# Solved blocks turned ahead of the second gap, and three solves begun ahead of the third: a recurrent-attention and mixture-of-experts kernel on one core

## The chip, the core and the metric

The kernel runs on one core of one Trainium2 chip. The metric is the device time of an execution in microseconds; three runs of the kernel before took 1157.42, 1158.74 and 1160.82 us, median 1158.74 us. The profile is one further execution, taken by the hardware profiler, with a span of 1155.3 us.

The engines are named as the profile names them: PE is TensorE (PEld its weight loads), DVE is VectorE, ACT is ScalarE, POOL is GpSimd, SP is SyncE, which issues most transfers. Each runs its own queue of instructions, and semaphores tie the queues together.

## The reference

Two blocks follow each other. The first is a recurrence over 768 time steps for 4 batches of 8 heads with a head size of 40:

```python
for t in range(S):
    y[:, :, t] = np.einsum('bhd,bhde->bhe', rt, state)
    Sa = np.einsum('bhde,bhe->bhd', state, at)
    state_decay = state * wt[:, :, None, :] - np.einsum('bhd,bhe->bhde', Sa, bt)
    state = state_decay + np.einsum('bhd,bhe->bhde', vt, kt)
```

Its output, reshaped to x of 3072 tokens by 320, goes through four experts of width 1024, whose results are mixed with normalized probabilities:

```python
p = domain_probs / (domain_probs.sum(-1, keepdims=True) + 1e-09)
for e in range(E):
    h = np.maximum(x @ w1[e], 0.0)
    out += p[:, e:e + 1] * (h @ w2[e])
```

All of it is in float32.

## The kernel before

The time axis is cut into 12 chunks of 64 steps. A **unit** is one chunk of two of the four batches; there are 24 units, two to a chunk, numbered from 0 here. Within a chunk the recurrence becomes matrix products and a triangular system, one of 64 by 64 for each head and batch. A unit goes through four generators, each cut into parts by `yield`:

- `within(q)`: everything that needs no state. Its parts in order: decay products G; the reciprocal gp; the scaled tokens n_tok and k_tok, the turned A, V and R (AT, VT, RT); NT and KT; the causal scores pc; the **triangle products** pfe, which give F (the strictly triangular matrix of the system) and the right side's ET; the copy into ET; EV.
- `substitute(q, engine)`: the **solve**. It gathers F's 32 by 32 diagonal blocks, turns them into M, makes the first products, and then substitutes row pair by row pair into Z, on POOL for all units from the third on.
- `merge(q)`: the **turning** of the solved blocks (Qc, QTc) and then the two products pY and pQ that join the blocks of 32 to one of 64.
- `step(q)`: the part that reads and writes the state, with the products prn, psat, pxr, pdy.

The parts of `within`, `substitute` and `merge` that matter here:

```python
        # within(q), sixth part: triangle products
        pf = quadrants(p, 0, BY_TOKENS, L, ...)          # pfe<-NT,AT
        pe = quadrants(p, NJ * L, BY_TOKENS, L, ...)     # pfe<-AT,KT
        q.F = sb.tile([P, H, L], FP32, name="F", tag="F", bufs=2)
        for s in range(2):
            nc.scalar.copy(out=of_slot(q.F[:], s), in_=pf[s])
        yield

    def substitute(q, eng, between=None):
        blocks = sb.tile([P, H, Q], FP32, name="blocks")
        for i in range(P // Q):
            move = nc.scalar.copy if i >= 2 else nc.vector.tensor_copy
            tc.keep_in_program_order(move(out=blocks[quarter(i)], in_=q.F[...]))
        M = sb.tile([P, Q, Q], FP32, name="M")
        ins = nc.vector.transpose(out=M[:], in_=cols)
        tc.keep_in_program_order(ins)
        tc.keep_in_program_order(nc.vector.memset(on_diag, 0.0))
        ...                                  # two products on DVE, into Z and M, pinned
        for x in (0, 3) if at_once else (0,):
            tc.keep_in_program_order(eng.tensor_copy(out=Z[:, x], in_=unit_cols[:]))
        for j in range(0, Q, 2):             # 16 row pairs: one product, two sums each
            ins = eng.tensor_tensor(out=Z[:, 1:3, 0:n, j + 1:Q], ..., op=ALU.mult)
            ...
                for x in range(1, 3):
                    eng.tensor_tensor(out=z[:, 0], in0=z[:, 0], in1=z[:, x], op=ALU.add)

    def merge(q):
        tc.keep_in_program_order(nc.vector.transpose(out=dealt(Qc[:]), in_=q.Z))
        tc.keep_in_program_order(nc.vector.transpose(out=QTc..., in_=Qc...))
        q.QT = QTs()
        for i in range(P // Q):
            ins = nc.gpsimd.tensor_copy(out=q.QT[...], in_=QTc[quarter(i)])
            tc.keep_in_program_order(ins)
        yield
        ...                                  # pY<-QTc,F on PE, Yq on ACT
        yield
        ...                                  # pQ<-Yq,Qc on PE, QT on ACT
        yield
```

`keep_in_program_order` pins an instruction behind the one traced before it on the same engine. What isn't pinned may be moved by the scheduler that lays out each engine's queue when the kernel is built.

Between these run the **mixture pieces**, queued in `todo`: `up` (ph, then relu into hs), the products with the second weights (po, or p after a scheme with seven products of half size whose sums `a` are made by `add_h` on DVE), and the adds to the output tile `osb` on DVE. PSUM tiles of the mixture share three buffers (tag "mm"), those of the attention five (tag "big"). A **gap** is a place in a step where some of these pieces are put:

```python
    for u in range(1, NU):
        ...
        m, s_next = merge(units[u + 1]), begin_step(u + 1)
        w = ws[u + 2]                        # within of unit u + 2
        def gap(n, pieces=None):
            at = 4 * u + n
            run(sum_ops, sums_at.get(at, 0))
            mix((1 if at in sparse else 2) if pieces is None else pieces)

        run(w_next)
        run(s, 1)
        gap(0)
        early = u < 5
        if early:
            run(s, 1)
        run(w, 1)
        run(s)
        ...
        run(w, 1)
        gap(1)
        if not early:
            run(m, 1)                        # Qc, QTc of unit u + 1
        ...                                  # loads for unit u + 3
        run(w, 2)                            # NT, KT; causal scores
        if early:
            run(m, 1)
        else:
            run(s_next, 1)                   # prn
            run(m, 1)                        # pY
        gap(2)
        if not early:
            run(m, 1)
        run(w, 1)                            # triangle products
        if not early:
            run(s_next, 1)
        if u + 2 < NU:
            substitute(units[u + 2], nc.gpsimd)
        run(w, 1)                            # ET
        ...                                  # G of unit u + 3
        if early:
            run(m, 1)
            run(s_next, 1)
            run(m)
            gap(3, 1)
            run(s_next, 1)
            ...
        else:
            gap(3)
        s = s_next
```

Of the kernel before, what the change touches and what calls it, by code (L numbers as in the profile page):

```python
# [15 lines left out]
def kernel(  # L16
# [38 lines left out]
    nc = tc.nc  # L55
# [9 lines left out]
    NU = NC * B // 2  # L65
# [103 lines left out]
    units = []  # L169

    def begin(u):
        q = Unit()
        q.u, q.c, q.bp = u, u // (B // 2), u % (B // 2)
        q.b = [2 * q.bp, 2 * q.bp + 1]
        q.start, q.end = q.c == 0, q.c == NC - 1
        q.n = {}
        units.append(q)
        return q
# [38 lines left out]
    def go(moves, eng=None):  # L217
        for move in moves:
            move(eng or nc.sync)
# [99 lines left out]
    def quarter(q):  # L319
        return slice(Q * q, Q * q + Q)  # L320
# [190 lines left out]
# [5 lines that stand above are left out]
            tc.keep_in_program_order(move(out=blocks[quarter(i)], in_=q.F[quarter(i), :, quarter(i % 2)]))  # L516
        M = sb.tile([P, Q, Q], FP32, name="M")
        cols = blocks[:].rearrange("p h c -> p c h")[:, :, None, :].to_broadcast([P, Q, 4, H])
        ins = nc.vector.transpose(out=M[:], in_=cols)  # L519
        tc.keep_in_program_order(ins)  # L520


        pairs = M[:].rearrange("p (c two) r -> p c two r", two=2)
        on_diag = M[:].rearrange("p c r -> p (c r)")[:, Q + 1::2 * (Q + 1)]
        tc.keep_in_program_order(nc.vector.memset(on_diag, 0.0))

        Z = sb.tile([P, 4, Q // 4, Q], FP32, name="Z")
        q.Z = Z[:, 0]
        by_second = Z[:, 1:3].rearrange("p x k r -> p (x k) r")
        below = M[:].rearrange("p c r -> p (c r)")[:, 1::2 * (Q + 1)]  # L530
        ins = nc.vector.tensor_tensor(
            out=by_second, in0=pairs[:, :, 1, :], in1=below[:, :, None].to_broadcast([P, Q // 2, Q]), op=ALU.mult,
        )
        tc.keep_in_program_order(ins)
        ins = nc.vector.tensor_tensor(out=pairs[:, :, 0, :], in0=pairs[:, :, 0, :], in1=by_second, op=ALU.add)  # L535
        tc.keep_in_program_order(ins)
        run(between)
        at_once = eng is nc.vector
        for x in (0, 3) if at_once else (0,):
            tc.keep_in_program_order(eng.tensor_copy(out=Z[:, x], in_=unit_cols[:]))  # L540
        for j in range(0, Q, 2):
            n, m = j // 4 + 1, Q - 1 - j
            here = 3 * (j // 2 % 2) if at_once else 0
            ins = eng.tensor_tensor(  # L544
                out=Z[:, 1:3, 0:n, j + 1:Q], in0=M[:, j:j + 2, None, j + 1:Q].to_broadcast([P, 2, n, m]),
                in1=Z[:, here, 0:n, j:j + 2].rearrange("p k x -> p x k")[:, :, :, None].to_broadcast([P, 2, n, m]),
                op=ALU.mult,
            )
            if j == 0:
                tc.keep_in_program_order(ins)  # L550
            z = Z[:, :, 0:n, j + 1:Q]
            if at_once:
                terms = z[:, 0:3] if here == 0 else z[:, 1:4]
                eng.tensor_reduce(out=z[:, 3 - here], in_=terms.rearrange("p x k r -> p k r x"), op=ALU.add, axis=AX.X)
# [3 lines that stand above are left out]
        if at_once:  # L558

            odd, even = (Z[:, x].rearrange("p k (r four) -> p k r four", four=4)[:, :, :, 1:3] for x in (3, 0))  # L560
            eng.tensor_copy(out=even, in_=odd)

    def merge(q):


        Qc = sb.tile([P, H, Q], FP32, name="Qc", tag="q", bufs=2)
        QTc = sb.tile([P, H, Q], FP32, name="QTc", tag="q", bufs=2)
        tc.keep_in_program_order(nc.vector.transpose(out=dealt(Qc[:]), in_=q.Z))
        tc.keep_in_program_order(
            nc.vector.transpose(  # L570
                out=QTc[:].rearrange("p h r -> p (h r)"), in_=Qc[:].rearrange("p h c -> p (h c)"),
            )
        )
        q.QT = QTs()
        for i in range(P // Q):
            ins = nc.gpsimd.tensor_copy(out=q.QT[quarter(i), :, quarter(i % 2)], in_=QTc[quarter(i)])  # L576
            tc.keep_in_program_order(ins)
        yield

        py = big("pY")  # L580
        for h in range(H):
            for i in (1, 3):
                nc.tensor.matmul(
                    out=py[quarter(i - 1), h * Q:(h + 1) * Q], lhsT=q.F[quarter(i), h, 0:Q],
                    rhs=QTc[quarter(i), h, :], start=True, stop=True,
                )
        Y = sb.tile([P, H, Q], FP32, name="Yq")
        for i in (0, 2):
            nc.scalar.copy(out=Y[quarter(i)].rearrange("p h t -> p (h t)"), in_=py[quarter(i), 0:H * Q])
        yield  # L590

        pq = big("pQ")
        for h in range(H):
            for i in (0, 2):
                nc.tensor.matmul(  # L595
                    out=pq[quarter(i), h * Q:(h + 1) * Q], lhsT=Qc[quarter(i), h, :],
                    rhs=Y[quarter(i), h, :], start=True, stop=True,
                )
        for i in (0, 2):
            nc.scalar.copy(out=q.QT[quarter(i), :, quarter(1)], in_=by(pq[quarter(i), 0:H * Q], Q))  # L600
        yield
# [301 lines left out]
    def begin_later(n):  # L903
        for move in later[:n]:
            tc.keep_in_program_order(move(nc.sync))
        del later[:n]

    def mix(n):

        for piece in todo[:n]:  # L910
            piece()
            begin_later(3 if n > 1 else 6)
        del todo[:n]

    def run(gen, n=99):
        if gen is None:
            return
        for _ in range(n):
            if next(gen, gen) is gen:
                break  # L920
# [3 lines left out]
    def begin_step(u):  # L924
        q = units[u]
        if q.bp == 0:
            chunks_x[q.c] = sb.tile([P, 3, 2 * P], FP32, name="xT", tag="xT", bufs=2)
        q.xT = chunks_x[q.c][:, :, q.bp * P:(q.bp + 1) * P]
        return step(q, q.xT)
# [91 lines left out]
    for u in range(1, NU):  # L1021
        q = units[u]
        m = s_next = w = w_next = iter(())
        if u + 1 < NU:
            m, s_next = merge(units[u + 1]), begin_step(u + 1)
            w_next = ws[u + 1]
        if u + 2 < NU:
            w = ws[u + 2]
# [16 lines that stand above are left out]
        if u == 1:  # L1045
            mixture_of_unit(q)
        elif q.bp:
            mixture_of_chunk(units[u - 1:u + 1], chunks_x[q.c])
        begin_later(len(later))
        run(w, 1)  # L1050
        gap(1)
        if not early:
            run(m, 1)

        if u + 3 < NU:
            go(load_raw(begin(u + 3), "WA"))
            load(units[u + 3], "WBKV")
            later.extend(load_raw(units[u + 3], "VR"))
        run(w, 2)
        if early:  # L1060
            run(m, 1)
        else:
            run(s_next, 1)
            run(m, 1)
        gap(2)

        if not early:
            run(m, 1)
        run(w, 1)
        if not early:  # L1070
            run(s_next, 1)
        if u + 2 < NU:
            substitute(units[u + 2], nc.gpsimd)
        run(w, 1)
        if u + 3 < NU:
            ws.append(within(units[u + 3]))
            run(ws[u + 3], 1)
# [6 lines that stand above are left out]
            mix(0 if 4 * u + 3 in sparse else 1)  # L1084
# [3 lines that stand above are left out]
# [31 lines left out]
```

## Time and profile before

| | |
|---|---|
| median of 3 runs | 1158.74 us (1157.42 to 1160.82) |
| span of the profiled execution | 1155.3 us |
| mean granted TensorE clock | 0.984 |
| DVE waiting for POOL's solve, before Qc | 6.7 us in 3 waits |
| POOL waiting for M, before a solve | 312.3 us in 20 waits |

How the views are read. The page's first line gives each engine's busy time, its share of the span and its instructions. A line of waits reads: engine, tile and line that waited, `<-` what it waited for, then the total in us, the number of times and the longest. A line of a timeline reads: start in us, duration in us, engine, line of the kernel, operation, out `<-` in, partitions by elements, and how many were merged; in brackets stands the idle time of the engine just before, and what ended it. L371 is a helper that issues all products of 64 by 64, so those are told apart by their tiles.

### The profile page before, as it was taken

What the parts mean: (1) busy time and instruction counts of PE and PEld (TensorE: products, weight loads), DVE (VectorE), ACT (ScalarE), POOL (GpSimd) and SP (SyncE); (2) the same over time, 40 slices, a digit from 0 to 9 for tenths busy, and PEclk for the clock granted to TensorE, in tenths of its full rate; (3) what the DMA queues carried; (4) which work ended last, traced back from release to release, by engine and by line L of the source; (5) the groups of instructions that cost most, each with busy time, mean ns of one, the idle gap of its engine ahead of it and who ended that gap; (6) DMA issues with size and microseconds to landing.
All of it is one profiled execution on the core that took longest, in us unless ns stands there. A gap on an engine that the chain in (4) does not pass through costs nothing.

```text
span 1155.3 us, 38242 instructions
## 1 busy us (share of the span) xinstructions
PE 1103.2 (95%) x16036; PEld 979.6 (85%) x16036; DVE 757.6 (66%) x1553; ACT 341.3 (30%) x860; POOL 471.9 (41%) x1221
## 2 busy tenths in 40 slices
PE   6899997999999999999999999999999999999998
PEld 5777776888898888988888888888989888888887
DVE  8756547697677758757667667677577586543333
ACT  2323333333233232242332332332322323311110
POOL 4005627672633634625525526426336346340000
PEclk7899998999999999999999999999999999999999
DMA  7774643254364354454443443443543442231330
GB/s 120 215 227 125 133 97 77 69 126 101 77 149 95 89 125 113 103 121 104 108 118 80 122 115 84 117 97 87 134 104 88 114 110 62 75 89 52 104 91 12
DMA packets 268866, 122.16 MB, mean 106 GB/s; under 512 B 213736, under 2 KB 242072, under 8 KB 268696
## 3 DMA queue, kind: packets, MB, share of 16 engines
q1 hardware_dynamic: 265416, 119.12, 42.1%
q8 instruction: 126, 2.06, 0.8%
q10 hardware_dynamic: 3280, 0.61, 0.3%
q14 instruction: 44, 0.36, 0.1%
HBM read 111.79 MB, written 3.93 MB: 100 GB/s over the span
## 4 chain that ended last, share of the span: by engine, by line
PE 68%; DVE 17%; SPq 4%; POOL 3%; issue 3%; DMA 3%; ACT 2%; DVEq 0%; ACTq 0%; POOLq 0%
PE ph L734 24%; PE p L841 22%; PE ph L726 7%; DVE osb L752 3%; POOL Z L557 2%; PE pfe L371 2%; PE psat L371 2%; PE pxr L371 2%; SPq L711 2%; PE pdy L371 2%; PE po L775 2%; DVE gp L414 1%; DVE G L401 1%; SPq L205 1%; DVE a L835 1%
## 5 line engine op out<-in xcount | busy, mean ns | idle before, releaser
L734 PE MATMUL ph<-xT,w1p 128*128 128x256 f32 (+1 forms) x1520 | 343.8, 379 | 0.7 <-issue 0.7
L734 PEld LDWEIGHTS ph<-xT,w1p 128*128 128x128 f32 x1520 | 274.0, 190 | 63.6 <-issue 24.7
L544 POOL TENSOR_TENSOR Z<-M,Z 128x62 f32<-128x62 f32 (+7 forms) x352 | 144.6, 411 | 344.9 <-DVE M L535 312.3
L557 POOL TENSOR_TENSOR Z<-Z 128x31 f32<-128x31 f32 (+7 forms) x704 | 258.6, 367 | 55.2
L835 DVE TENSOR_TENSOR a<-hs 128x512 f32<-128x512 f32 x220 | 152.7, 711 | 156.7 <-ACT hs L739 156.7
L739 ACT ACTIVATE hs<-ph 128x512 f32<-128x512 f32 (+1 forms) x208 | 117.1, 564 | 325.1 <-PE ph L734 325.0
L841 PE MATMUL p<-sums,a 128*128 128x160 f32 x1056 | 165.1, 299 | 0.0
L752 DVE SCALAR_TENSOR_TENSOR osb<-p,gate,osb 128x320 f32<-128x320 f32 (+1 forms) x243 | 108.1, 482 | 85.0 <-PE p L841 80.5
L841 PEld LDWEIGHTS p<-sums,a 128*128 128x128 f32 x1056 | 152.9, 190 | 2.3
L726 PE MATMUL ph<-xT,w1p 64*128 64x256 f32 (+1 forms) x760 | 110.3, 398 | 0.9 <-issue 0.9
L576 POOL COPY QT<-QTc 32x256 f32<-32x256 f32 x96 | 46.9, 488 | 154.8 <-DVE QTc L570 151.0
L841 PE MATMUL p<-w,hs 128*128 128x160 f32 x704 | 102.9, 299 | 0.0
L841 PE MATMUL p<-w,a 128*128 128x160 f32 x704 | 102.8, 299 | 0.0
L841 PEld LDWEIGHTS p<-w,hs 128*128 128x128 f32 x704 | 100.3, 190 | 2.2
L841 PEld LDWEIGHTS p<-w,a 128*128 128x128 f32 x704 | 98.0, 190 | 0.0
L726 PEld LDWEIGHTS ph<-xT,w1p 64*128 64x128 f32 x760 | 68.0, 187 | 13.7 <-issue 3.8
L519 DVE STREAM_TRANSPOSE M<-blocks 128x1024 f32<-128x1024 f32 x24 | 47.0, 1957 | 24.2 <-ACT blocks L516 24.1
L414 DVE RECIPROCAL gp<-gp 128x320 f32<-128x320 f32 x24 | 51.7, 2152 | 0.8
L504 ACT COPY EV<-pev 64x160 f32<-64x160 f32 x96 | 23.4, 286 | 66.8 <-PE pev L371 66.4
L600 ACT COPY QT<-pQ 32x256 f32<-32x256 f32 x48 | 17.4, 363 | 85.0 <-PE pQ L595 84.4
L371 PE MATMUL pdy<-VC,k_tok 64*64 64x104 f32 (+1 forms) x768 | 41.4, 260 | 0.1
L371 PE MATMUL pdy<-SX,n_tok 64*64 64x104 f32 (+1 forms) x768 | 38.9, 247 | 1.1 <-DVE SX L382 1.1
(148 smaller groups left out, 1347.3 us busy)
## 6 DMA issues: line engine op xcount, KB each, us to landing
w1p<-in_moe_w_dram SPq DMA_DIRECT2D x95, 512.0 KB
w1p<-in_moe_w_dram SPq DMA_DIRECT2D x190, 64.0 KB
w<-in_moe_w_dram SPq DMA_DIRECT2D x4, 1280.0 KB
sums<-in_moe_w_dram SPq DMA_DIRECT2D x9, 512.0 KB
natW<-in_w_dram SPq DMA_DIRECT2D x48, 80.0 KB
natB<-in_b_dram SPq DMA_DIRECT2D x48, 80.0 KB
natK<-in_k_dram SPq DMA_DIRECT2D x48, 80.0 KB
out_dram<-osb SPq DMA_DIRECT2D x46, 80.0 KB
```

Of the source, the lines that this page charges most:

```text
L371: nc.tensor.matmul(out=p[row][half(col), lo + at * out_cols:lo + (at + 1) * out_cols], lhsT=lhsT, rhs=rhs, start=(n == 0), stop=(n == len( ...
L414: pin(nc.vector.reciprocal(out=gp[:], in_=gp[:]))
L519: ins = nc.vector.transpose(out=M[:], in_=cols)
L544: ins = eng.tensor_tensor(out=Z[:, 1:3, 0:n, j + 1:Q], in0=M[:, j:j + 2, None, j + 1:Q].to_broadcast([P, 2, n, m]), in1=Z[:, here, 0:n, j: ...
L557: eng.tensor_tensor(out=z[:, 0], in0=z[:, 0], in1=z[:, x], op=ALU.add)
L576: ins = nc.gpsimd.tensor_copy(out=q.QT[quarter(i), :, quarter(i % 2)], in_=QTc[quarter(i)])
L726: nc.tensor.matmul(out=ph[i][:, f, :], lhsT=w1.last[i * DT:(i + 1) * DT, f, :], rhs=xT[i * DT:(i + 1) * DT, 2, :], start=(f == 0), stop=False,
L734: nc.tensor.matmul(out=ph[i][:, f, :], lhsT=w1.main[:, g, at * P:(at + 1) * P], rhs=xT[:, g, :], start=False, stop=(g == 1 and f == HF // ...
L739: nc.scalar.activation(out=h[:, i * HF // 2:(i + 1) * HF // 2, 0:n], in_=ph[i][:], func=ACTF.Relu,)
L752: nc.vector.scalar_tensor_tensor(out=to, in0=p, scalar=sc, in1=to, op0=ALU.mult, op1=ALU.add)
L835: nc.vector.tensor_tensor(out=t[:], in0=x, in1=y, op=op)
L841: nc.tensor.matmul(out=p[:, n * HD:(n + 1) * HD], lhsT=a[:, f, :], rhs=b[:, f, :], start=(f == 0), stop=(f == HF - 1),)
```

## The change

Two things are moved in the loop over u; no instruction is added or taken away.

- From u = 5 on, the turning of unit u + 1's solved blocks (`run(m, 1)`: Qc and QTc on DVE, then the copies into QT on POOL) is traced ahead of the second gap's mixture pieces instead of behind them.
- In the steps u = 2, 3 and 4, the triangle products of unit u + 2 and the begin of its solve (units 4, 5 and 6, the fifth to seventh) are traced ahead of the third gap's mixture pieces instead of behind them.

It is meant to have the solved blocks ready when pY asks for them. The whole diff:

```diff
@@ -1048,28 +1048,35 @@
             mixture_of_chunk(units[u - 1:u + 1], chunks_x[q.c])
         begin_later(len(later))
         run(w, 1)
-        gap(1)
         if not early:
             run(m, 1)
+        gap(1)
 
         if u + 3 < NU:
             go(load_raw(begin(u + 3), "WA"))
             load(units[u + 3], "WBKV")
             later.extend(load_raw(units[u + 3], "VR"))
         run(w, 2)
+
+        soon = u in (2, 3, 4)
+        if soon:
+            run(w, 1)
         if early:
             run(m, 1)
         else:
             run(s_next, 1)
             run(m, 1)
+        if soon:
+            substitute(units[u + 2], nc.gpsimd)
         gap(2)
 
         if not early:
             run(m, 1)
-        run(w, 1)
+        if not soon:
+            run(w, 1)
         if not early:
             run(s_next, 1)
-        if u + 2 < NU:
+        if not soon and u + 2 < NU:
             substitute(units[u + 2], nc.gpsimd)
         run(w, 1)
         if u + 3 < NU:
```

## The prediction

> **What bounds the kernel now.** I read the page's first part, then TensorE's own waits, then the timelines of TensorE (PE), VectorE (DVE) and GpSimd (POOL) around one late and one early solve.
>
> ```profile
> PE 1103.2 (95%) x16036; PEld 979.6 (85%) x16036; DVE 757.6 (66%) x1553; ACT 341.3 (30%) x860; POOL 471.9 (41%) x1221
> ```
>
> PE is busy for 1103.2 of 1155.3 us. Nothing but PE work or PE's idle time can move the end, and all its idle time together is 52 us, the start included. PE's waits (total, times, longest):
>
> ```profile
> PE pY L583 <- DVE QTc L570: 20.9, 21, 4.9
> PE pev L371 <- DVE ET L382: 6.6, 2, 5.8
> PE psat L371 <- issue: 3.1, 3, 1.4
> PE ph L726 <- DVE osb L750: 1.9, 1, 1.9
> ```
>
> One wait stands out, 21 times: the first product of `merge` (pY) waits for QTc, the solved block that DVE turns twice (Qc, QTc). This is the late pattern, for unit 13 in step u = 12; the first two lines are PE, then DVE in its order, last the end of POOL's solve:
>
> ```profile
> 581.71 0.67 PE L371 MATMUL prn<-ident,state 64*64 64x64 f32 x32
> 583.31 0.69 PE L583 MATMUL pY<-QTc,F 32*32 32x32 f32 x32 [0.93 <-DVE QTc L570]
> ...
> 577.14 0.70 DVE L223 STREAM_TRANSPOSE RT<-rawR 128x512 f32<-128x512 f32 x1
> 577.76 0.88 DVE L223 STREAM_TRANSPOSE G<-rawW 128x256 f32<-128x256 f32 x2
> ...
> 580.45 1.01 DVE L750 TENSOR_SCALAR osb<-p,gate 128x320 f32<-128x320 f32 x2
> 581.37 0.67 DVE L752 SCALAR_TENSOR_TENSOR osb<-p,gate,osb 128x160 f32<-128x160 f32 x2
> 581.96 0.61 DVE L568 STREAM_TRANSPOSE Qc<-Z 128x256 f32<-128x256 f32 x1
> ...
> 582.75 0.41 DVE L570 STREAM_TRANSPOSE QTc<-Qc 128x256 f32<-128x256 f32 x1
> ...
> 578.37 0.52 POOL L557 TENSOR_TENSOR Z<-Z 128x8 f32<-128x8 f32 x2
> ```
>
> The solve is done at 578.89, yet Qc starts at 581.96: 3.07 us later. In between DVE does the second gap's four adds to osb, which themselves waited for PE, because Qc is pinned behind them in program order. PE has finished prn at 582.38 and stands for 0.93 us. The early pattern is another one (unit 4, step u = 3):
>
> ```profile
> 188.19 0.65 PE L371 MATMUL pfe<-AT,KT 64*64 64x64 f32 x32
> 193.70 1.06 PE L583 MATMUL pY<-QTc,F 32*32 32x32 f32 x32 [4.86 <-DVE QTc L570]
> 194.69 1.09 PE L371 MATMUL prn<-state,AT 64*64 64x40 f32 x32
> ...
> 192.08 0.61 DVE L568 STREAM_TRANSPOSE Qc<-Z 128x256 f32<-128x256 f32 x1 [4.11 <-POOL Z L557]
> ...
> 191.53 0.51 POOL L557 TENSOR_TENSOR Z<-Z 128x8 f32<-128x8 f32 x2
> ```
>
> Here the solve itself is late: DVE waits 4.11 us for POOL, PE 4.86 us for DVE. Afterwards a 32-matmul group takes 1.06 us instead of 0.69: the windows view gives a granted clock of 0.50 for 193.70 to 200.00, 0.65 for 199.60 to 202.00 and 1.00 after it.
>
> [...] 0.50 after the 4.86 us gap, 1.00 in the steady stretches where gaps are 0.9 us. [...] a Qc that waits for POOL holds every DVE instruction behind it; the 4.11 us at 192.08 agrees. [...] the same solve takes 21.7 us in units 10 to 22 but 26.2 us in unit 6 (239.15 to 265.37), when DVE is fuller (35.2 us busy of 231 to 270, against 31.5 of 538 to 583).
>
> **The change part by part.** It adds and removes no instruction; two groups of work are moved. (The scheduler may still move unpinned instructions, but Qc, QTc, the block copies and M are pinned to their predecessor on DVE.)
>
> *Step 1: the turning ahead of the second gap's pieces, from u = 5.* Qc is now pinned behind RT instead of behind the four adds. For unit 13: RT ends at 577.84, Z at 578.89, so Qc 578.89 to 579.5 (0.61) and QTc to about 579.95 (0.41 and a small gap). PE asks for QTc at 582.38, 2.4 us later, so the whole 0.93 us goes. The waits of units 6 to 23, read from pY's lines, are 0.48, 0.49, 0.74, 0.94, 0.95, 0.86, 0.90, 0.93, 0.91, 0.87, 0.90, 0.88, 0.89, 0.87, 0.89, 0.88, 0.48, 0.55: together 14.4 us. One stays in part: unit 8's solve ends at 357.01, so QTc comes at about 358.1 where PE has pY at 358.41 now, and some 0.4 us remains. Sum: **14.0 us**.
>
> *Step 2: what DVE pays.* If Qc is queued right behind RT, DVE stands until Z is ready: 1.05 us for unit 13, 3.4 us for unit 9 (397.74 to 401.09), 3.7 us for unit 8 (353.3 to 357.01). G (2.5 us) and the adds (1.7 us) follow Qc, so the adds of unit 13 end near 584.2 instead of 582.0. Their PSUM buffer is next wanted by the products p at 588.55, RH by psat at 594.6. For unit 9 the same sum puts the adds' end at 406.3, and p is wanted at 407.5: a margin of 1.2 us, the thinnest. I take **0 us** on PE.
>
> *Step 3: triangle products and begin of the solve ahead of the third gap, u = 2, 3, 4.* Only a solve that PE waits for can pay, so unit 4's (begun in u = 2). Now its M is finished at 169.44, 6.0 us after QTc ends (163.41), since a sum of weights (0.78), two ET copies (0.44 each), half of G (0.42) and an RH addition lie in between. Block copies 0.67, M 1.92, memset 0.07, and two products of 0.69 make 4.0 us, so M could be done about 2 us earlier. POOL is free by 166.25 (QT copies 2.25, begin of Z 0.40), so it follows. But the products pfe (1.3 us) run ahead of the gap, can push pc and with it QTc back by up to 1.1 us, and leave PE without filler while it waits for unit 3's QTc (0.95 us now). So unit 4's solve ends 1 to 2 us earlier and the gap of 4.86 us shrinks to 3 or 4 us. The half clock costs about 3.8 us: 0.65 over 199.6 to 202.0 means that it ends near 201.3, and half of 193.7 to 201.3 is 3.8. A shorter gap may or may not escape it. I book **3 us**, out of 0 to 8.7 (4.86 and 3.8). Units 5 and 6 gain about 2 to 3 us of solve time that PE doesn't wait for; for unit 6 this keeps the turning of step 1 from stopping DVE.
>
> Sum: 1158.74 - 14.0 - 3 = about **1142 us**, 1.5% faster.
>
> **The rivals.** *A, POOL takes the place of the adds:* Qc stands in DVE's queue, the adds and `add_h` come late and PE waits for a free PSUM buffer or for the sums a. For it: POOL's end is within 0.8 us of Qc for units 8 and 9[...]. Against it: the margins of step 2, and that DVE is busy 66%. If it cost a microsecond in each of 18 units the time would be near 1158. *B, the scheduler keeps Qc behind the adds*, because its own timing has POOL finish later: then only step 3 remains, 1154 to 1158 us. Against it: for units 2 and 4 it queued Qc 2.40 and 4.11 us before the solve was done, so it takes POOL for faster than it is. *C, step 3 cures unit 4's wait wholly*, clock included: 8.7 us in place of 3, 1136 us. Against it: the chain from QTc to M alone gives 2 us. *D, another wait behind pY:* the third gap's ph comes 0.9 us earlier and could meet a weight transfer; PE's waits show none for w1p above 1.0 us in total, so I give it little.
>
> **Range and chances.** C at its best with all of step 1 gives 1135 to 1136, the 2% line; A or B in part give 1150. So 1135 to 1151 for 8 in 10, 1142 in the middle. Faster by over 2% needs 23.2 us, that is C and everything else: 0.06. Slower by over 2% needs a new stall of over a microsecond in each unit: 0.02.
>
> **What would show it.** Step 1: PE's wait for QTc falls from 20.9 us to 2 to 5 us, and Qc stands directly behind RT, or behind an idle time put down to POOL of 1 to 4 us, ahead of the osb adds; the steady period of a unit falls from 44.5 us (Qc at 581.96 and 626.48) to 43.6 us. Step 2: PE shows no new wait of over 2 us in sum for osb, a or AT. Step 3: the gap before unit 4's pY is 3 to 4 us; the clock in the slice near 190 us tells whether the penalty is gone. It is wrong if Qc still follows the adds, if PE waits on DVE's osb or a in each unit, or if in the early steps pY or psat waits longer since pfe no longer fills the wait.

## The result, and the profile after

The changed kernel took 1143.29 us (median of 4 runs, 1141.67 to 1146.21) against 1158.08 us (1156.54 to 1160.82) for the kernel before on the same chip: a ratio of 0.9873, with a 95% interval of 0.9845 to 0.9900. The prediction said 1142 us, 1135 to 1151.

The engine shares on the page of the kernel after:

```profile
PE 1102.2 (97%) x16036; PEld 979.1 (86%) x16036; DVE 758.5 (67%) x1553; ACT 338.1 (30%) x860; POOL 473.6 (42%) x1221
```

PE's busy time is the same within 1.0 us; what became less is its idle time, from 52 to 37 us. PE's own waits in the kernel after (total, times, longest):

```profile
PE pev L371 <- DVE ET L382: 6.6, 2, 5.8
PE pY L583 <- DVE QTc L570: 5.4, 3, 3.5
PE psat L371 <- issue: 2.9, 3, 1.6
PE pxT L699 <- DVE Y L687: 2.2, 1, 2.2
```

The wait for QTc fell from 20.9 us in 21 times to 5.4 us in 3, all of them before the first late unit (units 3, 4 and 5: 0.96, 3.48 and 0.99 us). Unit 13 again, from the timelines of PE, DVE and POOL of the kernel after:

```profile
574.69 0.67 PE L371 MATMUL prn<-ident,state 64*64 64x64 f32 x32
575.30 0.69 PE L583 MATMUL pY<-QTc,F 32*32 32x32 f32 x32
...
570.00 0.70 DVE L223 STREAM_TRANSPOSE RT<-rawR 128x512 f32<-128x512 f32 x1
571.77 0.63 DVE L568 STREAM_TRANSPOSE Qc<-Z 128x256 f32<-128x256 f32 x1 [1.07 <-POOL Z L557]
...
572.58 0.40 DVE L570 STREAM_TRANSPOSE QTc<-Qc 128x256 f32<-128x256 f32 x1
...
575.16 1.01 DVE L750 TENSOR_SCALAR osb<-p,gate 128x320 f32<-128x320 f32 x2
...
571.22 0.52 POOL L557 TENSOR_TENSOR Z<-Z 128x8 f32<-128x8 f32 x2
```

Qc now stands right behind RT. DVE is held for 1.07 us until POOL's solve ends at 571.74, and starts Qc 0.03 us later instead of 3.07 us. QTc is done at 572.98, pY is asked for at 575.30 and PE no longer stands. The adds to osb follow at 575.16. Over the run, DVE's wait for POOL ahead of Qc grew from 6.7 us in 3 times to 35.9 us in 19, and in the late units none of it reached PE: PE's waits list osb with 1.5 us (1.9 before) and neither a nor AT.

Unit 4, the early one:

```profile
191.69 1.07 PE L583 MATMUL pY<-QTc,F 32*32 32x32 f32 x32 [3.48 <-DVE QTc L570]
192.69 1.09 PE L371 MATMUL prn<-state,AT 64*64 64x40 f32 x32
...
190.46 0.61 DVE L568 STREAM_TRANSPOSE Qc<-Z 128x256 f32<-128x256 f32 x1 [2.96 <-POOL Z L557]
```

The gap is 1.4 us shorter in this execution, and the groups after it still take 1.07 and 1.09 us: the windows view gives a clock of 0.50 for 191.70 to 200.00.

Where the time came from can be read off pY's start times alone, which cut the execution into stretches:

| stretch | before | after |
|---|---|---|
| start to pY of unit 2 (both parts of the change come later) | 119.02 | 117.31 |
| pY of unit 2 to pY of unit 6 (step 3's part) | 150.68 | 150.46 |
| pY of unit 6 to pY of unit 23 (step 1's part) | 758.27 | 743.80 |

The late stretch gave 14.5 us, the early one 0.2 us. The first row, 1.7 us, lies ahead of everything that was moved and is the scatter of two single executions; behind pY of unit 23 the two differ by 0.5 us. The profiles of the experiments below show how far the other rows scatter. The late stretch takes 743.5 to 745.7 us in the seven with the new late order and POOL's late solves as they were, and 758.3 and 758.8 us in the two with the old one. The early stretch takes 150.5 to 153.0 us in the four with the new early order, and 150.7 to 151.9 us in the three with the old one. So the late gain is 13 to 15 us, and no early gain shows.

### The profile page after: what moved, and what is told of

It reads as the page before. It is cut to its first block, busy times and chain, and to the rows that moved or that the text cites. A ratio compares the mean times of both kernels' runs of the same rounds, so it can differ in the third digit from the quotient of the medians.

```text
span 1139.4 us, 38243 instructions
## 1 busy us (share of the span) xinstructions
PE 1102.2 (97%) x16036; PEld 979.1 (86%) x16036; DVE 758.5 (67%) x1553; ACT 338.1 (30%) x860; POOL 473.6 (42%) x1221
## 3 DMA queue, kind: packets, MB, share of 16 engines
HBM read 111.79 MB, written 3.93 MB: 102 GB/s over the span
## 4 chain that ended last, share of the span: by engine, by line
PE 88%; DVE 5%; POOL 2%; issue 2%; ACT 1%; DMA 1%; SPq 1%; DVEq 0%; ACTq 0%; POOLq 0%
PE ph L734 30%; PE p L841 28%; PE ph L726 9%; PE pdy L371 4%; PE po L775 2%; PE pfe L371 2%; PE psat L371 2%; PE pxr L371 2%; PE prn L371 2%; PE pQ L595 1%; PE pc L371 1%; PE pY L583 1%; PE pev L371 1%; POOL Z L557 1%; PE pg L335 1%
## 5 line engine op out<-in xcount | busy, mean ns | idle before, releaser
L734 PE MATMUL ph<-xT,w1p 128*128 128x256 f32 (+1 forms) x1520 | 345.0, 380 | 1.8 <-issue 1.7
L734 PEld LDWEIGHTS ph<-xT,w1p 128*128 128x128 f32 x1520 | 274.7, 191 | 65.3 <-issue 27.0
L557 POOL TENSOR_TENSOR Z<-Z 128x31 f32<-128x31 f32 (+7 forms) x704 | 255.7, 363 | 55.2
L835 DVE TENSOR_TENSOR a<-hs 128x512 f32<-128x512 f32 x220 | 152.5, 710 | 127.4 <-ACT hs L739 127.4
L576 POOL COPY QT<-QTc 32x256 f32<-32x256 f32 x96 | 49.3, 513 | 111.6 <-DVE QTc L570 99.9
L626 ACT COPY SN<-prn 128x256 f32<-128x256 f32 x44 | 15.5, 370 | 84.7 <-DVE RH L621 82.3
```

Source lines behind the costliest of these rows:

```text
L734: nc.tensor.matmul(out=ph[i][:, f, :], lhsT=w1.main[:, g, at * P:(at + 1) * P], rhs=xT[:, g, :], start=False, stop=(g == 1 and f == HF // ...
L835: nc.vector.tensor_tensor(out=t[:], in0=x, in1=y, op=op)
```

## The experiments

**The first part alone.**

```diff
-        soon = u in (2, 3, 4)
+        soon = False
```

> Only the first part of the change: the turning (Qc, QTc) ahead of the second gap from u = 5 on; the begin of the solves stays behind the third gap everywhere. Theory (the late turning is nearly the whole gain; between pY of unit 6 and pY of unit 23 the two profiles differ by 14.5 us): 1143 to 1145 us, TensorE's wait for QTc falls to about 6.5 us in 3 waits (0.95, 4.86 and 0.65, units 3 to 5). Rival (the earlier begin is needed, as prediction's step 3 has it, 3 us and a solve of unit 6 that doesn't stop VectorE): 1146 to 1148 us.

Measured: 1145.94 us, ratio 0.9883 (0.9859 to 0.9907), against 0.9873 for the whole change: the intervals lie over each other. Its late stretch is 745.3 us and its early one 151.0. PE waits for QTc 7.1 us in 4 times: the three expected ones, and 0.67 us at unit 8. VectorE's wait for unit 6's solve, which the earlier begin was to remove, is 2.62 us here, and still 2.25 us in the kernel after. Here that solve ended at 266.27 and Qc began at 266.31, but QTc was still ready well ahead of pY at 271.00, and PE didn't stand there.

**The second part alone.** The kernel after, with `gap(1)` back in front of `run(m, 1)`.

> Only the second part: triangle products and begin of the solve ahead of the third gap in u = 2, 3 and 4; the turning stays behind the second gap. Theory (the begin gains about 0.4 us on unit 4's solve and gives it back in other waits): 1157 to 1159 us, the wait of unit 4's pY about 3.5 us instead of 4.9, another early wait longer by as much, and the clock still at half after it. Rival (step 3 of the prediction): 1155 us.

Measured: 1158.68 us, ratio 1.0002 (0.9990 to 1.0013). The interval leaves a gain of 1.2 us at most for step 3, which I had booked with 3. Unit 4's pY waits 4.62 us, not the 3.5 of my theory, and PE's wait for QTc is nearly what it was before:

```profile
PE pY L583 <- DVE QTc L570: 20.5, 21, 4.6
```

So the first part is the whole gain, as far as these runs can tell.

**Taking PE's wait away from the other side.** The kernel before, with pY behind the third gap from u = 5 on:

```diff
         else:
             run(s_next, 1)
-            run(m, 1)
         gap(2)
         if not early:
             run(m, 1)
         run(w, 1)
         if not early:
+            run(m, 1)
             run(s_next, 1)
```

> The kernel before, with the first join product pY moved behind the third gap's pieces from u = 5 on (pQ behind the triangle products); the turning stays where it was. It takes TensorE's wait away from the other side. Theory (the gain is TensorE's 0.9 us per unit of standing before pY and nothing else): the wait for QTc in units 6 to 23 is gone and the time is 1143 to 1146 us, if pQ doesn't wait for Yq. Rival 1 (a wait of pQ for Yq of 0.5 to 1 us takes its place): 1152 to 1158 us. Rival 2 (what counts is the earlier QTc on VectorE and GpSimd, not TensorE's wait): 1158 us with no wait for QTc left.

Measured: 1159.94 us, ratio 1.0015 (1.0002 to 1.0027). No late pY waits any more, yet nothing is gained. My theory's time is off, and so is the first rival, since pQ waits no longer than before (1.1 us in all). The time is that of the second rival, but PE's timeline of one unit gives another reason:

```profile
597.99 0.65 PE L371 MATMUL pfe<-AT,KT 64*64 64x64 f32 x32
598.56 0.69 PE L595 MATMUL pQ<-Yq,Qc 32*32 32x32 f32 x32
599.18 0.70 PE L726 MATMUL ph<-xT,w1p 64*128 64x256 f32 x4
...
601.24 0.70 PE L726 MATMUL ph<-xT,w1p 64*128 64x256 f32 x4
601.88 3.72 PE L734 MATMUL ph<-xT,w1p 128*128 128x256 f32 x16
```

PE never idles in this unit (44.20 us busy of 44.20 in the windows view), so that no earlier QTc could have shortened it. But pQ now comes so late, as I read the order, that psat, which needs its copies, lands in the middle of ph's first group. From the end of the products p to L734 the same work, pY included, takes 5.03 us (596.85 to 601.88); in the kernel after it takes 3.76 (584.98 to 588.74) and pY's 0.62, 4.38 in all. So 0.65 of the 0.9 us turned from idle into a longer sequence of small products: the period is 44.2 us, against 44.5 before and 43.6 after. The remaining 0.3 us or so a unit were lost again at single units. pY of unit 6 to pY of unit 7 takes 49.5 us against 44.3, with a gap of 1.99 us before psat and the clock at 0.50 for some 6 us after it, and units 8, 9, 20 and 21 take 3.3 us more together. A wait that is gone from the list is not yet time gained.

**How much slack the new order has.** In the kernel after, 5 or 10 idle copies (128x256, 0.40 us each) were put into POOL's solve of units 7 to 23, and 10 into the kernel before. The edit in short, with 10 copies:

```diff
+            [tc.keep_in_program_order(eng.tensor_copy(out=Z[:, 3], in_=unit_cols[:]))
+             for _ in range(10 if j == 16 and q.u > 6 else 0)]
```

> The kernel after, with five idle copies (128x256, 0.40 us each, 2.0 us in all) put into GpSimd's solve of units 7 to 23; they write a part of Z that nothing reads. The queues of the other engines keep their order. Theory (QTc of a late unit is ready some 2.3 us before TensorE asks for it, except in units 7 to 10): almost nothing in units 11 to 23, 1 to 2 us each in units 7 to 10: 1145 to 1151 us. Rival (VectorE held by Qc for 2 us longer delays the adds and the sums, prediction's rival A): 2 us per unit, about 1175 us.

> The kernel after, with ten such copies (4.0 us) in the solves of units 7 to 23. Theory (the ring from QTc over the third gap, the triangle products, M and the solve back to QTc has some 2.3 us of slack in a period of 43.6 us): 1.7 us per unit, 17 units, about 1172 us, with QTc the wait of TensorE. Rival (slack is larger, GpSimd idles 343 us waiting for M): below 1150 us.

> The kernel before, with the same ten copies (4.0 us) in the solves of units 7 to 23. Theory (the adds hide 3.07 us of a longer solve there, then the same ring sets the period): 0.9 us per unit more, about 1172 us, equal to the kernel after with the same copies within 3 us: the change gains nothing once the solve is 4 us longer. Rival (the change's gain doesn't depend on the solve's length): 15 us above the kernel after with the copies.

Measured: 1148.28 us with 5 copies (ratio 0.9912, 0.9886 to 0.9937), 1168.33 with 10 (1.0079, 1.0052 to 1.0106), and 1187.25 for the kernel before with 10 (1.0245, 1.0224 to 1.0267). The solve grows by less than the copies' own time: 5 lengthen it from 21.7 to 23.0 us, 10 to 24.4 us, in the kernel before to 25.2 us.

The first two bear the theory out: 1.3 us more solve is absorbed in nearly all units (unit 8 waits 1.88 us, unit 23 0.51, the others not), 2.7 us more is not. With 10 copies the period goes from 43.6 to 45.1 us, and the ring, in which each part waits for the one before, closes: pY to the solve's first step 19.3, solve 24.4, its end to pY 1.4, together 45.1. In the kernel after itself the same ring reads 18.7 (575.30 to 594.02) and 21.7, and the solve ends 3.12 us before the next pY (615.73 and 618.85), of which Qc, QTc and the hand-over need 1.4: 1.7 us of slack, not the 2.3 I had taken from QTc's end.

The third disproves it. I expected the kernel before to meet the kernel after once the solve bounds both; it stayed 19 us behind. Two lines, unit 13 of the kernel before with the copies and unit 14 after it, and the windows view of 8 us behind each such pY:

```profile
598.29 0.69 PE L583 MATMUL pY<-QTc,F 32*32 32x32 f32 x32 [1.60 <-DVE QTc L570]
...
643.64 0.69 PE L583 MATMUL pY<-QTc,F 32*32 32x32 f32 x32 [1.73 <-DVE QTc L570]
644.26 1.25 PE L726 MATMUL ph<-xT,w1p 64*128 64x256 f32 x8
645.44 4.82 PE L734 MATMUL ph<-xT,w1p 128*128 128x256 f32 x14
```

```profile
598.30:606.30 8.00, 8.00 (x77) 1.00 0.62 144
643.60:651.60 8.00, 7.96 (x64) 0.79 0.51 128
```

(Columns: the stretch, its length, PE's busy time and count, granted clock, DMA share, GB/s.) PE's gap before pY is mostly 1.6 to 1.7 us in this kernel, and mostly 0.8 to 0.9 in the kernel after with the copies. In about every second unit the clock then falls: 0.79 over 8 us is 3.4 us at half rate, 1.7 us lost. Its periods mostly alternate between 45.3 and 47.0 us, where the other kernel's are 45.0 to 45.2. Eight such falls, in units 8 to 20, cost some 15 us, as unit 10's is twice as long. The kernel after with the copies has three (units 7, 8 and 23, behind gaps of 1.43, 1.51 and 1.68 us), which cost some 5 us. So the clock makes some 10 of the 16 us by which the two profiles differ (spans of 1185.1 and 1168.7 us). The rest goes with a period that is 0.3 us longer between the falls: the solve takes 0.8 us more, pY to its first step 0.5 us less. Unit 13's solve shows where the 0.8 us lie (two lines of the kernel before with the copies, then one of the kernel after with them):

```profile
593.59 1.41 POOL L557 TENSOR_TENSOR Z<-Z 128x35 f32<-128x35 f32 x2
593.72 1.23 DVE L401 TENSOR_TENSOR_SCAN G<-G,first 128x512 f32<-128x512 f32 x1
...
585.62 0.62 POOL L557 TENSOR_TENSOR Z<-Z 128x35 f32<-128x35 f32 x2
```

One pair of POOL's sums meets DVE's scan of G, takes 1.41 us instead of 0.62 and ends 0.05 us behind the scan. In the kernel after with the copies DVE stands at Qc at that time, and its scan comes later. The 13 solves of units 9 to 21 in the kernel before with the copies all show this; of the other 31 solves of both kernels none meets the scan in this pair, and 30 take 0.61 to 0.69 us for it.

**The early stretch: four attempts to move it.** Step 3 had promised 3 us there and gave nothing, so I looked for what bounds it. On the kernel after, the state's products prn ahead of pY in u = 2 to 4:

```diff
         if early:
+            if soon:
+                run(s_next, 1)
             run(m, 1)
-            run(s_next, 1)
+            if not soon:
+                run(s_next, 1)
             run(m)
```

> The kernel after, with the state's products prn traced ahead of pY in u = 2, 3 and 4 (as they are from u = 5 on). They fill 1.2 us of TensorE's 3.48 us gap before unit 4's pY. Theory (the half clock from 191.7 to 201.3 us is set off by that one gap[...]): 5 us off, 1.2 of the gap and 3.8 of the clock, 1138 to 1139 us, the clock at 1.00 throughout that stretch. Rival (the clock falls all the same): 1142 us. Rival 2 (prn only moves the wait to psat): 1143 us.

Measured: 1144.01 us, ratio 0.9873 (0.9848 to 0.9898). The gap was still 3.13 us: prn of u = 2 had moved ahead of unit 3's pY as well, so that PE's work between the two joins was no longer than before and was done as early. The clock fell all the same (0.50 from 196 to 200 us), as the first rival had it; that a shortened gap would leave it up was my estimate, and isn't shown (one of 2.29 us, below, didn't). Next, the mixture piece behind the join of u = 3 in front of it (`if u == 3: gap(3, 1)` ahead of `run(m, 1)`):

> The kernel after, with the mixture piece that stands behind unit 4's join in u = 3 traced ahead of it, so that its 4.8 us of products fill TensorE's 3.48 us gap before pY. Theory (gap and half clock both go, but the filler is then missing where psat waits for RH and QT): 3 to 5 us off, 1138 to 1140 us, with a new wait of 2 to 4 us before psat. Rival (no gain, since the wait only moves and the clock falls there): 1143 us.

Measured: 1146.49 us, ratio 0.9898 (0.9872 to 0.9923). Nothing is gained, as the rival had it. The gap before pY is gone and stands before psat instead, longer than in my theory:

```profile
194.27 0.69 PE L595 MATMUL pQ<-Yq,Qc 32*32 32x32 f32 x32
204.65 0.51 PE L371 MATMUL psat<-QT,RH 64*64 64x64 f32 x5 [9.68 <-DVE RH L621]
```

psat waits for RH, which DVE makes at 204.19, behind M, G and the sums a. So prn and RH were traced ahead of the turning and the begin of the solve in u = 2 to 4 (`run(s_next, 1)` right behind the triangle products), once alone and once with the piece in front:

> The kernel after, with the state's products prn and their sums RH of u = 2, 3 and 4 traced ahead of the turning and the begin of the solve, so that VectorE makes RH while it would otherwise stand for GpSimd, and M follows QTc with less in between. Theory (the early steps are bound by VectorE's queue from QTc over M to RH, in which the earlier begin only changed places with RH): unit 4's solve starts 1 us earlier, psat no longer waits for RH, 2 to 5 us off, 1139 to 1141 us. Rival (the early steps are bound by GpSimd's solve of 21 to 23 us alone): TensorE's gap before unit 4's pY stays above 2 us with the half clock after it, and the time stays at 1142 to 1145 us.

> The same, and the mixture piece of u = 3 ahead of unit 4's pY, as in the run before that put the piece first and only moved the gap to psat (9.7 us for RH). Theory (that gap was RH behind M on VectorE, nothing else): no gap before pY, one of 1 to 3 us before psat for the copies of QT, no half clock near 200 us, 4 to 8 us off, 1135 to 1139 us. Rival (the filler is missing further on, where pdy and Y wait for VectorE behind M): the gaps only move again and the time stays at 1142 to 1146 us.

Measured: 1143.28 us, ratio 0.9870 (0.9850 to 0.9890), and 1145.57 us, ratio 0.9893 (0.9873 to 0.9913). Both times are the rivals'. In the first, psat no longer waits for RH, but the gap before unit 4's pY is still 2.29 us with the clock at 0.50 behind it, and unit 4's solve starts no earlier (6.15 us behind pY of unit 3, against 5.64 in the kernel after). In the second, pY and psat no longer wait long, and the loss turns up further on, where PE stands around pg and pdy, and at half clock behind them (2.08 us for a group of 1.13, as at the clock of 0.50 in the kernel before, at 197.60):

```profile
203.78 0.55 PE L335 MATMUL pg<-ident,G 128*128 128x128 f32 x3
205.97 0.43 PE L371 MATMUL pdy<-SX,n_tok 64*64 64x104 f32 x1 [1.65 <-DVE SX L382]
...
206.51 0.47 PE L335 MATMUL pg<-ident,G 128*128 128x128 f32 x1
...
209.88 2.08 PE L726 MATMUL ph<-xT,w1p 64*128 64x256 f32 x8
```

From pY of unit 2 to pY of unit 6 the stretch is 150.7 us before, 150.5 after, 151.7, 152.5, 151.9 and 153.4 in these four. The kernels after with 5 and 10 copies, whose early part is that of the kernel after, take 152.5 and 153.0 us, so these four don't stand out from the scatter, and no order of the same work shortened the stretch. The last run therefore took work out: the kernel after without the last eight of sixteen row pairs in the solves of units 3 to 6, so that its output is no longer the reference's.

```diff
-        for j in range(0, Q, 2):
+        for j in range(0, 16 if q.u in (3, 4, 5, 6) else Q, 2):
```

> The kernel after, with the last eight of the sixteen row pairs left out of GpSimd's solve of units 3 to 6 (the output isn't the reference's; what is left out is half of those solves, some 10 us of GpSimd for each). Everything else is as in the kernel after. Theory (the stretch from pY of unit 2 to pY of unit 6, 150.5 us in both kernels and 151 to 153 us in every rearrangement, is bound by other things than the solve, so that a wait taken away comes back elsewhere): TensorE's gap before unit 4's pY goes, the stretch gets 0 to 3 us shorter, 1141 to 1144 us. Rival (the solve of unit 4 bounds it, and an earlier begin only didn't reach far enough): 3.5 us of the gap and 3.8 us of the half clock go, the stretch falls to about 143 us, 1136 us.

Measured: 1137.87 us, ratio 0.9812 (0.9781 to 0.9843). Unit 4's solve takes 13.0 us instead of 23.0, and:

```profile
189.81 0.69 PE L583 MATMUL pY<-QTc,F 32*32 32x32 f32 x32 [0.43 <-DVE QTc L570]
190.43 0.68 PE L371 MATMUL prn<-state,AT 64*64 64x40 f32 x32
```

The clock stays at 1.00 in every window from 184 to 202 us, and the stretch falls to 145.1 us, 5.3 to 7.9 less than in the four profiles with the same early order and whole solves. The ratios, 0.9812 against 0.9873, say some 7 us, give or take 5. This is nearer to the rival (7.3 us) than to my theory (0 to 3). The early stretch does hang on the solve: what was missing in step 3 was reach, not effect. Counted from pY of unit 3, unit 4's solve ends after 28.6 us in the kernel after, after 28.3, 28.7, 27.7 and 27.7 in the four attempts, and after 18.6 in this run: the attempts mostly chose where PE would wait for it.

## Why the prediction was right, point by point

- **Step 1** was right in mechanism and size: 14.0 us predicted, 13 to 15 us in the late stretch, with 0.9883 for that part alone, and the period fell from 44.5 to 43.6 us as forecast. PE's wait for QTc fell to 5.4 us, just above the forecast 2 to 5, as the early waits stayed. The stated order (Qc behind RT, held by POOL for about a microsecond) is there for unit 13: 1.05 us predicted, 1.07 seen. The remainder of 0.4 us named for unit 8 appears with the first part alone (0.67 us), not with both. One reading was wrong. Of unit 13's 3.07 us the adds take only the last 1.5 (from 580.45); DVE works on G ahead of them. In units 9 to 21 no idle time stands before the adds, so they did not hold DVE up by waiting for PE there; in units 6 to 8, 22 and 23 they did, by 1.7 to 6.4 us. That Qc was queued behind them, which the step rests on, is right.
- **Step 2** held: DVE pays 35.9 us of waiting, and in the late units PE pays none of it. Rival A needed the queue behind Qc to be late by more than the adds' slack. With 5 copies more it still isn't, with 10 it is QTc itself that comes late, not the adds.
- **Step 3** is the term that was mis-sized: 3 us booked, no gain beyond the scatter in the profiles, at most 1.2 by the run of that part alone. The failing step is "M could be done about 2 us earlier", and with it "unit 4's solve ends 1 to 2 us earlier". From QTc's end to the end of M it is 6.03 us before (163.41 to 169.44) and 5.55 after (161.75 to 167.30):

```profile
161.67 0.41 DVE L382 COPY_PREDICATED ET<-mask_up,pfe 128x256 f32<-128x256 int32 x1
...
163.23 1.96 DVE L519 STREAM_TRANSPOSE M<-blocks 128x1024 f32<-128x1024 f32 x1
165.11 0.41 DVE L223 STREAM_TRANSPOSE G<-rawW 128x256 f32<-128x256 f32 x1
165.46 0.31 DVE L621 TENSOR_TENSOR RH<-prn,EV 128x160 f32<-128x160 f32 x1
```

  Of the five things that lay in between only the sum of weights left, because only that was pinned; ET, G and RH are unpinned, and the scheduler put them in again. Moving the trace of M doesn't empty the queue ahead of it. The solve then starts 0.5 us earlier (5.64 us behind pY of unit 3 instead of 6.12), takes 0.5 us longer (23.0 instead of 22.5) and ends where it did, 28.6 us behind that pY. All four profiles with each early order agree in this within some 0.1 us; why the solve takes longer isn't shown. That unit 4's gap measured 3.48 us, inside the forecast 3 to 4, is luck: the three other profiles with the new early order have 3.50, 4.62 and 4.63 us, the four with the old one 3.93 to 4.86. And PE waits longer elsewhere in all four: pxT 2.2 us (0.9 with the old order) and unit 5's pY 0.99 (0.65). So the total came within 1.3 us of the 1142 because step 1, nearly the whole of it, was right.
- **The clock.** I said that a shorter gap may or may not escape the half clock. It didn't at 3.48, 3.13 or 2.29 us: the granted clock was 0.50 behind each. How short a gap would have to be was not shown.
- **Rivals B and D** are out: Qc left the adds in every late unit, and among the late units ph has one new gap without a visible cause, of 0.89 us (at 854.96). **Rival C** was right that the early gap and its clock are worth several microseconds, but they are not had by this change: the run with the shortened solves shows 5.3 to 7.9 us of them.

## What to carry to other kernels

When one engine is 95% busy and its largest wait is short but comes in every round, look at what stands in the producer's queue between the data being ready and the instruction that takes it: here the work on G and four adds, none of which the waiting engine needed as soon. Letting a side engine stand a microsecond for its input, ahead of work that can be late, was worth more here than keeping it busy. But a wait that leaves the list is only time gained if no longer sequence and no later wait takes its place, so measure from round to round, and test an order that didn't help by taking work away before giving the cause up.

## What the runs showed of the hardware that I had not expected

- The clock fell to half after gaps far shorter than the 4.86 us before unit 4's pY in the kernel before. In the kernel before with 10 copies the seven gaps of 1.71 to 1.81 us before pY in units 8 to 20 were followed by half clock (unit 14's of 1.73 us by 0.79 over 8 us), and those of 1.60 to 1.64 us were not (1.00 behind unit 13's of 1.60). But the length of one gap doesn't decide it: one of 1.56 us was followed by half clock there and one of 1.53 us was not, and in the kernel after with 10 copies those of 1.43 and 1.51 us were. In unit 3 the first psat waits 1.45 us in the kernel before and 1.46 us in the two kernels built on it that share its early order (pY behind the third gap, and the copies); the clock stayed at 1.00 in the first and fell to 0.50 in the other two. The time at half rate, worked out from the clock over 8 us (0.79 in seven of the eight falls, 0.57 in unit 10), was 3.4 us in the seven and 6.9 us in unit 10. What sets the half clock off, these runs don't show.
- One pair of GpSimd's sums, 0.62 us by itself, took 1.41 us in all 13 solves in which VectorE's scan of 1.23 us came beside it, and ended 0.05 to 0.07 us behind the scan. So where VectorE's queue had this instruction made GpSimd's chain 0.8 us longer here (25.2 us against 24.4); why the pair takes longer beside it isn't shown.
